# A convolution in the transform domain: two GpSimd sums wait for a later VectorE instruction

## The chip, the cores and the metric

The kernel runs on one core of a Trainium2 chip. A core has five engines, each with its own queue of instructions: TensorE (matmuls and the loads of their stationary operand; PE and PEld in the profile), VectorE (DVE), ScalarE (ACT), GpSimd (POOL) and SyncE (SP, which here only issues DMAs). Engines wait for each other through semaphores: a counter that an instruction raises when it is done, and that another engine's instruction waits for at a given value. The metric is the device time of one execution in microseconds, as the median of several executions.

## The reference

The input x is one image of 224 x 224 pixels with 96 channels, w is a 7 x 7 kernel from 96 to 96 channels, both in bf16. The reference pads w to 224 x 224, transforms both along height and width, multiplies per frequency over the channels, and transforms back:

```python
wp = jnp.pad(w, ((0, H - K), (0, W - K), (0, 0), (0, 0)))
Xf = rfft2(x.astype(float32), axes=(1, 2))
Wf = rfft2(wp.astype(float32), axes=(0, 1))
Yf = jnp.einsum('bhwi,hwio->bhwo', Xf, Wf)
y = irfft2(Yf, s=(H, W), axes=(1, 2)).astype(bfloat16)
```

This is a circular convolution of the image with the 7 x 7 kernel.

## The kernel before

The height is cut into 8 blocks of 28 rows (`NJ`, `B`), the width into 7 tiles of 32 pixels. Along the height a block is taken into a short transform with 17 pairs of components (`NS`), by matmuls with the matrix `Fm`; the result is `xf`. The weights are taken into the same transform by matmuls with `wq`; the result is `WF`, in slots of three parts for each pair: the first two, and their difference, which VectorE makes (`diff` in `prep_jobs`, one bf16 subtraction of 96 x 960 for each pair). Along the width the convolution stays direct, in a form that makes two output columns at a time out of differences and sums of the even and odd columns, the planes `J`. A burst of three VectorE instructions (`jit`) makes the planes of up to three pairs.

A round (t, s) makes the products of tile t for pair s (`b_round`). For an inner pair it is this. Nineteen matmuls into one PSUM bank, b0; ScalarE takes three fifths of it into `tt_`; VectorE takes the rest and makes `u`. Then come jobs of other stages (`mid`: matmuls for the weights or pixels of later rounds, their evictions, and the weight differences). Fourteen matmuls go into a second bank, b1, and VectorE makes `v` from it. Then come the round's plane burst, if it has one (`planes`), and at last the sum of v and u into `yf`, by GpSimd in most rounds:

```python
if not ydve:
    y = ysum(GE)
    if last is not None:
        tc.add_manual_dep(y.ins, last.ins.name, SYNC, reason="sum after planes")
```

The sum of a round with a burst so waits for the burst's last instruction, that of a round without one for its own v. The rounds with pair 0 and the last pair have a single VectorE instruction that writes `yf`, and no sum.

The first two tiles are worked on together: the second follows the first by four rounds (`LAG`). Around the change the order is (0,3), (0,4), (1,0), (0,5), (1,1): first-tile round 3 has a burst (buffer J_66 in the program), round (0,4) has three weight differences in its jobs, round (1,0) has a burst (J_64).

The order on each engine is written out by hand: a wrapper (`_Ordered`) ties each instruction to the one before it on its engine. The tiles u, v and `tt_` have two buffers each, so u of one inner round waits for the sum of the inner round two before it. PSUM has eight banks of 512 floats, handed out in turn as they are emptied; a group of matmuls waits for the eviction of the bank that it takes. `yf` holds three rounds and is stored by one DMA on SP's queue when the third sum is done.

All instructions that go through the wrapper carry its line (L88) in the profile, so that tiles' names and times tell them apart. By the tile of ScalarE's output, the rounds around the change are: (0,3) tt__920, (0,4) tt__1041, (1,0) tt__1107, (0,5) tt__1159, (1,1) tt__1240.

Of the kernel before, what the change touches and what calls it, by code (L numbers as in the profile page):

```python
# [38 lines left out]
JGB = ((0, 3), (3, 6), (6, 9), (9, 12), (12, 15), (15, 17))  # L39
# [5 lines left out]
FI = 6  # L45
LROUND = {8: 16, 11: 15}
WARM0 = 2
BIAS = 2000.0


# [5 lines left out]
def kernel(  # L56
# [18 lines left out]
    SYNC = mybir.DependencyInfo(mybir.DependencyClass.Sync, mybir.DependencyReason.DATA)  # L75
# [19 lines left out]
    VE, SE, GE, TE, DE = (_Ordered(e) for e in (nc.vector, nc.scalar, nc.gpsimd, nc.tensor, nc.sync))  # L95
# [426 lines left out]
        return ops  # L522

    yf_cur = {}

    def pairs(ap):
        return ap.rearrange("p (r g o) -> p g r o", r=2, o=2)
# [4 lines left out]
    def b_round(t, s, mid, end, ydve=False, planes=()):  # L532
        xf = xf_tiles[t][0:C]
        Jb = jbuf[(t, s)]
        xv = xf.rearrange("c p r s w j -> c p r s (w j)")
        st = {
            0: (Jb[:, 4], xv[:, 0, 1, s], xv[:, 0, 0, s]),
            1: (Jb[:, 6], Jb[:, 3], Jb[:, 2]),
            2: (Jb[:, 5], Jb[:, 1], Jb[:, 0]),
        }  # L540
        if t == TL:
            yt, i = (YA, 2 * s) if s < SA else (YB, 2 * (s - SA))
            ym = yt[:, :, i:i + 2, :].rearrange("p g r o -> p g (r o)")
        else:
            for (y0, y1) in YGRP:
                if s == y0:
                    yf_cur[t] = (yf_pool.tile([128, YMAX, 2, 2, C], BF16, name="yf"), y0, y1)
            yf, y0, y1 = yf_cur[t]
            ym = yf[:, s - y0].rearrange("p r m o -> p m r o")

        def conv(bank, col, m, part, add=False, both=False):
            pl = st[m][part] if s not in REAL else (xv[:, 0, :, s], Jb[:, 2:4], Jb[:, 0:2])[m][:, part]
            tp = TAPS[m]
            for k, tp_ in enumerate(tp):
                o, wv = bank[:, col:col + C], WF[0:C, slot(s, part), tp_, :]
                if both:
                    o, wv = bank[:, col:col + 2 * C].rearrange("p (m o) -> p m o", m=2), wv.unsqueeze(1).to_broadcast([C, 2, C])
                TE.matmul(o, lhsT=pl[:, (HALO - k) * NJ:(HALO - k) * NJ + 128], rhs=wv,
                          start=(k == 0 and not add), stop=(k == len(tp) - 1 and not both and m != 2 or not add and not both and k == len(tp) - 1))
        b0, b1 = bank(), bank()  # L560
        merge = t < 2 and s in MERGE
        tt_ = tv_pool.tile([128, 4 * C], F32, name="tt_")
        if s in REAL:
            for part in range(2):
                conv(b0, part * C, 0, part)
            if t == TL:
                SE.copy(out=tt_.rearrange("p (r m o) -> p r m o", r=2, m=2),
                        in_=b0[:, 0:2 * C].rearrange("p (r o) -> p r o", o=C).unsqueeze(2).to_broadcast([128, 2, 2, C]))
            else:
                SE.copy(out=tt_[:, 0:2 * C], in_=b0[:, 0:2 * C])  # L570
            mid()
            for mi, m in enumerate((2, 1)):
                for part in range(2):
                    conv(b1, (part * 2 + mi if t == TL else mi * 2 + part) * C, m, part)
            if t == TL:
                VE.tensor_tensor(out=yp(ym), in0=pairs(tt_[:]), in1=pairs(b1[:, 0:4 * C]), op=ALU.add)
            else:
                VE.tensor_tensor(out=ym,
                                 in0=tt_[:, 0:2 * C].rearrange("p (r o) -> p r o", o=C).unsqueeze(1).to_broadcast([128, 2, 2, C]),
                                 in1=b1[:, 0:4 * C].rearrange("p (m r o) -> p m r o", m=2, r=2), op=ALU.add)  # L580
            load["a"] += 110 + 0.9 * 192
            load["v"] += 540
            for f in planes:
                f()
            end()
        else:
            v = tv_pool.tile([128, 2, 2, C], F32, name="v")
            if merge:
                conv(b0, 2 * C, 0, 0, both=True)
                conv(b0, 2 * C, 2, 0, add=True)  # L590
                conv(b0, 3 * C, 1, 0, add=True)
                conv(b0, 0, 0, 1)
                conv(b0, C, 0, 2)
                SE.mul(out=tt_[:], in_=b0[:, 0:4 * C], mul=-0.5)
                u, pr = tt_[:, 2 * C:4 * C].rearrange("p (m o) -> p m o", m=2), tt_[:, 0:2 * C]
            else:
                for part in range(3):
                    conv(b0, part * C, 0, part)
                conv(b0, 3 * C, 2, 0)
                conv(b0, 4 * C, 1, 0)  # L600
                u = tv_pool.tile([128, 2, C], F32, name="u")
                if t == TL:
                    SE.mul(out=tt_[:, 0:C], in_=b0[:, 0:C], mul=-0.5)
                    SE.copy(out=tt_[:, C:3 * C], in_=b0[:, C:3 * C])
                    load["a"] += 240
                else:
                    SE.mul(out=tt_[:, 0:3 * C], in_=b0[:, 0:3 * C], mul=-0.5)
                pr = tt_[:, C:3 * C]
            if not merge:
                VE.scalar_tensor_tensor(out=u[:], in0=b0[:, 3 * C:5 * C].rearrange("p (m o) -> p m o", m=2), scalar=-0.5,  # L610
                                        in1=tt_[:, 0:C].unsqueeze(1).to_broadcast([128, 2, C]), op0=ALU.mult, op1=ALU.add)
            mid()
            for mi, m in enumerate((2, 1)):
                for pi, part in enumerate((1, 2)):
                    conv(b1, (pi * 2 + mi if t == TL else mi * 2 + pi) * C, m, part)
            if t == TL:
                VE.tensor_tensor(out=v[:], in0=pr.rearrange("p (r o) -> p r o", r=2).unsqueeze(2).to_broadcast([128, 2, 2, C]),
                                 in1=b1[:, 0:4 * C].rearrange("p (r m o) -> p r m o", r=2, m=2), op=ALU.add)
            else:
                VE.scalar_tensor_tensor(out=v.rearrange("p m r o -> p m (r o)"),  # L620
                                        in0=pr.unsqueeze(1).to_broadcast([128, 2, 2 * C]), scalar=-2.0,
                                        in1=b1[:, 0:4 * C].rearrange("p (m q) -> p m q", m=2), op0=ALU.mult, op1=ALU.add)
            def ysum(eng):
                if t == TL:
                    return eng.tensor_tensor(out=yp(ym), in0=pairs(v.rearrange("p r m o -> p (r m o)")),
                                             in1=u.rearrange("p m (g o) -> p (m g) o", o=2).unsqueeze(2).to_broadcast([128, C, 2, 2]), op=ALU.add)
                return eng.tensor_tensor(out=ym, in0=v[:],
                                         in1=u.unsqueeze(2).to_broadcast([128, 2, 2, C]), op=ALU.add)
            if ydve:
                ysum(VE)  # L630
            last = None
            for f in planes:
                last = f()
            if not ydve:
                y = ysum(GE)
                if last is not None:
                    tc.add_manual_dep(y.ins, last.ins.name, SYNC, reason="sum after planes")
            load["a"] += 490 if merge else 410
            load["v"] += (560 if ydve else 250 if t < 2 else 0) + (560 if merge else 900)
            end()  # L640
        if t != TL and s == y1 - 1:
            dma(scr_tiles[t].rearrange("w j s e -> (w j) s e")[:, y0:y1], yf[:, 0:y1 - y0].rearrange("p s r m o -> p s (r m o)"))
# [130 lines left out]
    last = [f() for f in fj[0][1]]  # L773
# [8 lines left out]
    tv_pool = ctx.enter_context(tc.tile_pool(name="tv", bufs=2))  # L782
    load["v"], load["a"] = BIAS, 0.0

# [25 lines left out]
    bursts = {}  # L810
# [7 lines left out]
    nburst = len(bursts)  # L818
    for r in range(NS + LAG):
# [31 lines left out]
        for t in range(2):  # L851
            s = r - LAG * t
# [3 lines left out]
            now = jit(*now) if now else ()  # L856
            both = LAG <= r < NS
            b_round(t, s, fills(qs, 2 * r + (t if both else 0)), fills(qs, 2 * r + (t if both else 1)), False, now)
    assert not bursts and nburst == 2 * len(JGB)
    if NP2:  # L860
        ps0_cm.__exit__(None, None, None)
        ps_cms = [tc.tile_pool(name="ps", bufs=NP2, space=bass.MemoryType.PSUM),
# [42 lines left out]
    turn_b()  # L905
    load["v"] = 2 * BIAS + load["a"]
    for f in cj:
# [20 lines left out]
    order = [(j, h) for j in range(NJ) for h in range(2)]  # L928
    warm(WARM0)
    live = {k: first(*k) for k in order[:FI]}  # L930
    LF = 4
    for i, (j, h) in enumerate(order):
# [3 lines left out]
        k = i + 8 - LF  # L936
# [38 lines left out]
```

## Time and profile before

| | us |
|---|---|
| median of 3 runs (lowest, highest) | 262.58 (261.45, 262.92) |
| the profiled execution, whole | 261.39 |
| its span, first to last instruction | 259.7 |
| TensorE busy in the span | 250.1 |
| VectorE busy | 213.8 |
| ScalarE busy | 197.9 |
| GpSimd busy | 107.8 |
| mean granted TensorE clock | 0.996 |

Times in the views are microseconds from the start of the span. A row of the timeline has the start, the time taken, the engine, the line, the operation, the tiles (out<-in), the shape, and how many instructions of a kind stand in the row; in brackets the engine's idle time before it and what ended that. Consecutive VectorE instructions overlap in the records by 0.08 us. A row of waits has who waited for whom, the total, the number of times and the longest.

### The profile page before, as it was taken

The numbers are of one execution on the slowest core, as the hardware profiler recorded it, in microseconds if no ns is written. First come the engines' busy times: TensorE is split into PE (matmuls) and PEld (weight loads), VectorE is DVE, ScalarE is ACT, GpSimd is POOL, SyncE is SP. The second block draws the span as 40 slices with busy tenths as digits, with TensorE's granted clock in tenths as the row PEclk, the third lists the DMA queues.
The fourth block names the chain that finished last, engine by engine and source line by source line (L and its number), as shares of the span: only waits on it lengthen the run. The fifth ranks groups of instructions, "written<-read, shape, count | busy, mean of one in ns | idle before, by whom it ended". The sixth has DMA issues, their size and how long they took to land.

```text
span 259.7 us, 12201 instructions
## 1 busy us (share of the span) xinstructions
PE 250.1 (96%) x5156; PEld 234.3 (90%) x5156; DVE 213.8 (82%) x455; ACT 197.9 (76%) x499; POOL 107.8 (42%) x172
## 2 busy tenths in 40 slices
PE   8999998999999999999999999999999999999981
PEld 3679998999999999999999998999999999999961
DVE  5649999798978979977988788777978889889982
ACT  5548997668875667998988879989798886666662
POOL 7784123336446543334133322543133332555621
PEclk9999999999999999999999999999999999999998
DMA  6947010731111299888979549697969853595145
GB/s 166 254 126 208 24 49 3 209 113 48 48 48 61 96 254 194 247 237 254 284 213 231 161 122 301 197 264 159 321 232 208 225 172 135 142 172 165 53 117 177
DMA packets 41416, 43.44 MB, mean 167 GB/s; under 512 B 30836, under 2 KB 33104, under 8 KB 41362
## 3 DMA queue, kind: packets, MB, share of 16 engines
q1 hardware_dynamic: 41044, 41.98, 58.7%
q8 instruction: 40, 0.66, 1.1%
q0 software_dynamic: 192, 0.52, 0.7%
q10 hardware_dynamic: 126, 0.17, 0.2%
q14 instruction: 14, 0.11, 0.1%
HBM read 22.09 MB, written 19.66 MB: 161 GB/s over the span
## 4 chain that ended last, share of the span: by engine, by line
PE 82%; DVE 6%; issue 4%; ACT 3%; POOL 3%; DVEq 0%; POOLq 0%; ACTq 0%
PE pb L88 82%; POOL ct L88 2%; DVE J L88 2%; ACT WF L88 1%; DVE xf L88 1%; DVE u L88 1%; POOL yf L88 1%; DVE v L88 1%; DVE WF L88 1%; ACT xf L88 1%; DVE wq L88 1%; DVE yf L88 0%; ACT tt L88 0%; ACT tt__1860 L88 0%; ACT tt__1159 L88 0%
## 5 line engine op out<-in xcount | busy, mean ns | idle before, releaser
L88 PE MATMUL pb<-WF,J 96*128 96x96 bf16 x2782 | 160.4, 206 | 0.1
L88 PEld LDWEIGHTS <-J 96*128 96x128 bf16 x2782 | 136.5, 98 | 7.0 <-issue 0.2
L88 POOL TENSOR_TENSOR yf<-v,u 128x384 bf16<-128x384 f32 x70 | 69.8, 1011 | 124.1 <-issue 67.8
L88 ACT CAST xf<-pb 96x408 bf16<-96x408 f32 (+2 forms) x147 | 68.8, 487 | 8.7 <-PE pb L88 6.9
L88 PE MATMUL pb<-WF,xf 96*128 96x96 bf16 x991 | 61.4, 206 | 0.8 <-ACT xf L88 0.5
L88 DVE TENSOR_TENSOR J<-xf 96x1824 bf16<-96x1824 bf16 (+1 forms) x82 | 56.8, 732 | 0.1
L88 PEld LDWEIGHTS <-xf 96*128 96x128 bf16 x991 | 48.9, 98 | 1.4 <-ACT xf L88 0.6
L88 PE MATMUL pb<-Fm,xn 118*128 118x136 bf16 (+3 forms) x640 | 45.5, 199 | 0.8 <-DVE u L88 0.8
L88 ACT CAST WF<-pb 96x480 bf16<-96x480 f32 (+1 forms) x57 | 28.4, 579 | 4.7 <-PE pb L88 4.6
L88 PE MATMUL pb<-tt,Gm 102*84 102x384 bf16 (+1 forms) x132 | 32.0, 325 | 0.0
L88 PEld LDWEIGHTS <-xn 118*128 118x128 bf16 x640 | 30.5, 97 | 1.1 <-issue 1.0
L88 ACT CAST yo<-pb 84x384 bf16<-84x384 f32 (+1 forms) x65 | 27.8, 484 | 2.8 <-PE pb L88 2.8
L88 ACT CAST J<-pb 84x384 bf16<-84x384 f32 (+1 forms) x65 | 28.0, 484 | 2.5 <-PE pb L88 2.5
L88 DVE TENSOR_TENSOR J<-J 96x912 bf16<-96x912 bf16 (+2 forms) x41 | 22.8, 556 | 0.0
L88 PE MATMUL pb<-wq 98*128 98x120 bf16 (+1 forms) x288 | 21.3, 226 | 0.2 <-DMA wq<-wq 0.2
L88 PEld LDWEIGHTS <-wq 98*128 98x128 bf16 x288 | 19.4, 148 | 0.7 <-issue 0.7
L88 POOL TENSOR_TENSOR xn<-v,u 128x384 bf16<-128x384 f32 x12 | 10.9, 925 | 9.2 <-DVE J L88 6.2
L88 DVE CAST WF<-pb 96x480 bf16<-96x480 f32 (+1 forms) x15 | 8.8, 614 | 4.2 <-PE pb L88 4.0
L88 PE MATMUL pb<-wu 128*128 128x512 bf16 x39 | 10.8, 438 | 1.1 <-DVE ct L88 1.1
L88 DVE TENSOR_TENSOR yf<-v,u 128x384 bf16<-128x384 f32 x20 | 11.2, 558 | 0.7
L88 PEld LDWEIGHTS <-Gm 102*84 102x84 bf16 (+1 forms) x132 | 11.4, 118 | 0.2
L88 ACT COPY xf<-xf 96x816 bf16<-96x816 bf16 (+3 forms) x18 | 10.3, 630 | 0.0
(406 smaller groups left out, 253.5 us busy)
## 6 DMA issues: line engine op xcount, KB each, us to landing
scr<-yf SPq DMA_DIRECT2D x30, 288.0 KB
xn<-in_x_dram SPq DMA_DIRECT2D x12, 672.0 KB
tt<-scr SPq DMA_DIRECT2D x24, 336.0 KB
out_dram<-yo SPq DMA_DIRECT2D x12, 252.0 KB
out_dram<-J SPq DMA_DIRECT2D x12, 252.0 KB
tt<-scr SPq DMA_DIRECT2D x6, 288.0 KB
WF<-in_x_dram SPq DMA_DIRECT2D x2, 672.0 KB
scr<-yf SPq DMA_DIRECT2D x6, 192.0 KB
```

Of the source, the lines that this page charges most:

```text
L88: r = fn(*a, **k)
```

## The change

Two of GpSimd's sums are emitted later in the program, and each waits for the VectorE instruction that was emitted last at that point. The sum of round (0,3) is emitted in round (0,4), behind the three weight differences, and waits for the last of them instead of the burst of its own round. The sum of round (0,4) is emitted in round (1,0), behind the burst, and waits for its last instruction instead of v of its own round. All other sums stay as they were. In the built program each engine has the same instructions in the same order as before; the values that these two sums wait for on VectorE's counter go from 69 to 74 and from 75 to 79, and nothing else differs.

```diff
+YLATE = {(0, 3): 0, (0, 4): 1}
...
+    later = []
+
+    def settle(kind):
+        for k, f in list(later):
+            if k == kind:
+                later.remove((k, f))
+                f(VE._last)
...
             mid()
+            settle(0)
...
             for f in planes:
                 f()
+            settle(1)
             end()
...
             mid()
+            settle(0)
...
             for f in planes:
                 last = f()
-            if not ydve:
+            settle(1)
+
+            def pool_sum(after):
                 y = ysum(GE)
-                if last is not None:
-                    tc.add_manual_dep(y.ins, last.ins.name, SYNC, reason="sum after planes")
+                if after is not None:
+                    tc.add_manual_dep(y.ins, after.ins.name, SYNC, reason="sum after VectorE")
+            if (t, s) in YLATE:
+                later.append((YLATE[(t, s)], pool_sum))
+            elif not ydve:
+                pool_sum(last)
```

More of the change, by code (lines that the diff above doesn't have):

```diff
@@ L858 @@
             b_round(t, s, fills(qs, 2 * r + (t if both else 0)), fills(qs, 2 * r + (t if both else 1)), False, now)
-    assert not bursts and nburst == 2 * len(JGB)
+    assert not bursts and nburst == 2 * len(JGB) and not later
     if NP2:
```

## The prediction

> **What bounds the kernel now.** I read the page first, then the waits of TensorE over the steady part, then the timeline around the two sums. The page, and the stretch of 53 to 247 us with busy time by engine (PE, PEld, DVE, ACT, POOL, each with its instruction count, then the granted clock, the DMA share and GB/s):
>
> ```profile
> span 259.7 us, 12201 instructions
> PE 250.1 (96%) x5156; PEld 234.3 (90%) x5156; DVE 213.8 (82%) x455; ACT 197.9 (76%) x499; POOL 107.8 (42%) x172
> 53.00:247.00 194.00, 193.53 (x4077) 185.54 (x4075) 164.71 (x349) 154.67 (x403) 79.40 (x84) 1.00 0.65 177
> ```
>
> TensorE is busy for 193.53 of the 194.00 us behind the place of the change, at a granted clock of 1.00. So TensorE's stream of matmuls sets the end, and a stall taken out of it earlier should arrive at the end nearly whole. Its waits between 36 and 247 us are one group, and its timeline shows the larger one (an idle time of the engine and what ended it stand in brackets):
>
> ```profile
> PE pb L88 <- DVE u L88: 1.1, 2, 0.8
> ```
>
> ```profile
> 41.83 0.92 PE L88 MATMUL pb<-wq 98*128 98x120 bf16 x12
> 43.51 0.95 PE L88 MATMUL pb<-Fm,xn 118*128 118x32 bf16 x32 [0.76 <-DVE u L88]
> ...
> 45.70 0.92 PE L88 MATMUL pb<-wq 98*128 98x120 bf16 x12
> 46.46 0.56 PE L88 MATMUL pb<-Fm,xn 118*128 118x32 bf16 x16
> ```
>
> Two waits make 1.1 us, and the one at 43.51 is 0.76 of it. The undisturbed pace stands two rows lower: from the twelve weight matmuls to the pixel matmuls behind them it is 46.46 - 45.70 = 0.76 us from start to start. By that pace the matmuls of 43.51 could have started at 41.83 + 0.76 = 42.59, so the stall costs at most 0.92 us. It ended on VectorE's u of first-tile round 5 (tile tt__1159), so VectorE and GpSimd before it are to be read:
>
> ```profile
> 37.42 0.34 DVE L88 SCALAR_TENSOR_TENSOR u<-pb,tt__1041 128x192 f32<-128x192 f32 x1
> 37.69 2.14 DVE L88 TENSOR_TENSOR WF<-WF 96x960 bf16<-96x960 bf16 x3
> 39.75 0.54 DVE L88 SCALAR_TENSOR_TENSOR v<-tt__1041,pb 128x384 f32<-128x384 f32 x1
> 40.22 0.54 DVE L88 TENSOR_TENSOR yf<-tt__1107,pb 128x384 bf16<-128x384 f32 x1
> 40.68 1.96 DVE L88 TENSOR_TENSOR J<-xf 96x1824 bf16<-96x1824 bf16 x2
> 42.56 0.62 DVE L88 TENSOR_TENSOR J<-J 96x912 bf16<-96x912 bf16 x1
> 43.11 0.34 DVE L88 SCALAR_TENSOR_TENSOR u<-pb,tt__1159 128x192 f32<-128x192 f32 x1
> 43.38 0.54 DVE L88 SCALAR_TENSOR_TENSOR v<-tt__1159,pb 128x384 f32<-128x384 f32 x1
> 43.84 0.34 DVE L88 SCALAR_TENSOR_TENSOR u<-pb,tt__1240 128x192 f32<-128x192 f32 x1
> 44.10 0.64 DVE L88 CAST WF<-pb 96x480 bf16<-96x480 f32 x1
> ```
>
> ```profile
> 37.18 1.00 POOL L88 TENSOR_TENSOR yf<-v,u 128x384 bf16<-128x384 f32 x1 [3.82 <-DVE J L88]
> 40.37 1.00 POOL L88 TENSOR_TENSOR yf<-v,u 128x384 bf16<-128x384 f32 x1 [2.19 <-DVE v L88]
> 43.99 1.00 POOL L88 TENSOR_TENSOR yf<-v,u 128x384 bf16<-128x384 f32 x1 [2.63 <-DVE v L88]
> ```
>
> VectorE has no idle time in these rows: it is behind, and every tenth it saves before 43.11 moves u forward. The first two GpSimd rows are the sums of first-tile rounds 3 and 4, the third is that of round 5. The sum of round 3 (37.18 to 38.18) lies over the weight differences that start at 37.69; that of round 4 (40.37 to 41.37) over the plane burst that starts at 40.68. What this does, taken apart in narrow windows:
>
> ```profile
> 37.69 1.01 DVE L88 TENSOR_TENSOR WF<-WF 96x960 bf16<-96x960 bf16 x1
> 38.62 0.64 DVE L88 TENSOR_TENSOR WF<-WF 96x960 bf16<-96x960 bf16 x1
> ...
> 28.96 1.10 DVE L88 TENSOR_TENSOR J<-xf 96x1824 bf16<-96x1824 bf16 x1
> ...
> 40.68 1.65 DVE L88 TENSOR_TENSOR J<-xf 96x1824 bf16<-96x1824 bf16 x1
> ...
> 51.86 1.02 DVE L88 TENSOR_TENSOR WF<-WF 96x960 bf16<-96x960 bf16 x1
> ...
> 235.86 1.22 DVE L88 TENSOR_TENSOR J<-xf 96x1824 bf16<-96x1824 bf16 x1
> ```
>
> ```profile
> 50.41 1.96 POOL L88 TENSOR_TENSOR yf<-v,u 128x384 bf16<-128x384 f32 x2 [3.65 <-DVE J L88]
> ...
> 235.20 0.92 POOL L88 TENSOR_TENSOR xn<-v,u 128x384 bf16<-128x384 f32 x1 [0.43 <-DVE xf L88]
> ```
>
> A difference takes 0.64 without a sum beside it and 1.01 at 37.69; the first burst instruction takes 1.10 alone (28.96) and 1.65 at 40.68. Overlap against excess in the four places: 38.18 - 37.69 = 0.49 against 0.37; 41.37 - 40.68 = 0.69 against 0.55; 52.37 - 51.86 = 0.51 against 0.38; 236.12 - 235.86 = 0.26 against 0.12. The excess is each time the overlap less 0.12 to 0.14: the VectorE instruction is held almost until the running sum ends. I use "overlap less 0.13".
>
> **The change part by part.** All engines keep their instructions and their order; two GpSimd sums wait for a later VectorE instruction. Nothing is added or removed, and no DMA moves in its queue.
>
> 1. The sum of round 3 leaves the weight differences: the first falls from 1.01 to 0.64 or 0.65, and VectorE gains 0.36 (the overlap of 0.49 less 0.13). The differences end at 37.69 + 2.14 - 0.36 = 39.47 instead of 39.83. A sum starts 0.08 after its release (v ends at 40.29, sum at 40.37), so it runs from 39.55 to 40.55.
>
> 2. What it now lies beside: v of round 4 (from 39.39) and the second tile's first yf (from 39.86), each with one operand in PSUM. The yf row of 40.22 lay beside a sum from 40.37 on and took 0.54, the same as v at 39.75, which ended before that sum began; so I price these two at nothing. If v were held to the moved sum's end, less the 0.13, it would end at 40.42 instead of 39.93 and the gain would fall by 0.49 to 0.32; no row has such an instruction held.
>
> 3. The burst starts at 40.68 - 0.36 = 40.32, with 40.55 - 40.32 = 0.23 of the moved sum still to run. By overlap less 0.13 that costs 0.10, near the 0.12 of the row at 235.86 with almost the same overlap. The ends are 0 and the whole 0.23. The sum of round 4 is gone from it (0.55). Net 0.45 in the burst, with ends of 0.32 and 0.55.
>
> 4. Together u of round 5 starts 0.36 + 0.45 = 0.81 sooner, at 42.30, and ends at 42.64 instead of 43.45. TensorE started 0.06 behind that end (43.51), so its pixel matmuls start at 42.70, 0.81 sooner and 0.11 above the 42.59 that its own pace allows. With the ends of step 3 the gain is 0.68 to 0.91, and the pace caps it at 0.92.
>
> 5. What waits for the moved sums. u of round 5 writes the buffer that the sum of round 3 reads: that sum ends at 40.55, u starts at 42.30, so 1.75 is to spare. u of second-tile round 1 (tt__1240) writes the buffer that the sum of round 4 reads. That sum is released by the burst's end, 43.18 - 0.81 = 42.37, and runs 42.45 to 43.45. VectorE is at this u at 43.84 - 0.81 = 43.03 and now stands idle to about 43.48, taking the 0.03 after a sum's end from this pair:
>
> ```profile
> 57.51 1.03 POOL L88 TENSOR_TENSOR yf<-v,u 128x384 bf16<-128x384 f32 x1 [1.95 <-issue]
> 58.57 0.36 DVE L88 SCALAR_TENSOR_TENSOR u<-pb,tt__1653 128x192 f32<-128x192 f32 x1 [0.47 <-POOL yf L88]
> ```
>
> That is a new wait of 0.45, yet u starts 0.36 sooner than before (43.48 against 43.84). Its PSUM bank is taken next by the weight matmuls of 45.70, which move to 44.89; u ends at 43.82, 1.07 earlier. Queued behind it is the weight eviction of 44.10, now 43.74 to 44.38, whose bank is wanted at 45.65 (46.46 less 0.81). So it costs nothing.
>
> 6. GpSimd's queue: behind the sum of round 4 stands that of round 5, at 43.45 instead of 43.99; the store of rounds 3 to 5 on SP's queue waits for this one and can go 0.54 sooner. ScalarE works from the same banks:
>
> ```profile
> 40.41 0.41 ACT L88 ACTIVATE tt__1159<-pb 128x288 f32<-128x288 f32 x1 [1.23 <-PE pb L88]
> 42.07 0.77 ACT L88 CAST xf<-pb 96x320 bf16<-96x320 f32 x2
> ```
>
> The activation of 40.41 follows v of round 4 (end 40.29) and moves forward 0.36 with it; the evictions of 42.07 end at 42.48, and TensorE wants their banks from 43.10 (half of the pixel matmuls behind 42.70). Nothing is late there.
>
> The sum: -0.81 us. The profiled execution took 261.39 us (1.69 outside its span) and would take 260.58. It lies 1.19 under the median of 262.58; set against the median the prediction is 261.8. That is 0.3%, and a measurement of this kernel can tell about 0.5% from no change.
>
> The Trainium skill's page "SBUF — State Buffer", section "Who interferes with whom", has a rule that speaks partly against the change: a VectorE instruction with two SBUF inputs and a GpSimd instruction that reads SBUF exclude each other, and whichever issues first keeps the port for its whole length. The trace agrees but for the 0.13. By the rule taken whole, the burst of step 3 loses 0.23 and the gain is 0.68; by the rows it is 0.81.
>
> **The rivals.** (a) The moved sum holds the burst for the whole 0.23: step 4 gives 0.68, 261.9 us. Against it stand the four rows that are 0.12 to 0.14 short. (b) No gain: VectorE's lead is used up elsewhere, for instance because the sum of round 3 starts late and lies wholly over the burst. At a start of 40.3 it would hold the burst for 0.87, u of round 5 would gain 0.36 + 0.55 - 0.87 = 0.04, and the time would be 262.5. For it speaks that the sum's end and the burst's start are only 0.23 apart; against it that the lag from release to start would have to be 0.8 where the rows show 0.08. (c) Slower: the sum of round 4, now last before u of tt__1240, becomes TensorE's wait. This decides once the sum ends past 43.45 + 1.07 = 44.52, and it is slower than before past 45.33. The longest of the 70 sums took 1670 ns:
>
> ```profile
> L88 POOL TENSOR_TENSOR yf<-v,u x70: 992/1000/1670, 31.1 to 220.3; 128x384 bf16<-128x384 f32 x70
> ```
>
> With that length it ends at 44.12, still in time. It needs a second such delay and 1.3 us more to be past the band; at an end of 46.0 the time would be 262.58 + 0.67 = 263.3.
>
> **How the numbers follow.** Forecast (gain 0.7 to 0.9) 0.66; (a) 0.12; (b) 0.14; (c) 0.08. The likeliest is 261.8; its own range is 261.6 to 262.1. The range reaches up to (b) and the highest run of before (262.9), and down to the profiled run less the cap, 261.39 - 0.92 = 260.5, since the runs of before spread from 261.45 to 262.92 and three new ones may gather at the fast end. Beyond 0.5% (1.31 us) no step leads; the scatter of two medians gives 0.16 of faster. Slower is (c), 0.08. Within the band is left 0.76.
>
> **What would show it.** Right: in the profile after, the first difference behind u of tt__1041 takes 0.64, the burst's first instruction 1.1 to 1.25, u of tt__1159 starts 0.7 to 0.9 sooner, TensorE's idle time of 0.76 is gone or under 0.15, and u of tt__1240 has a new wait of some 0.4 on GpSimd. Wrong: the burst still takes 1.6 (b), TensorE waits for u of tt__1240 (c), or the stall is gone and the span is not shorter, which would mean that a later stall takes it back.

## The result and the profile after

The changed kernel takes 260.68 us (median of 22 runs, 260.36 to 263.80) where the kernel before, run beside it, takes 261.75 us (22 runs, 260.98 to 263.33). The ratio is 0.9964, with a 95% interval of 0.9949 to 0.9978: 0.94 us less, between 0.58 and 1.33 (the plain difference of the two medians is 1.07). The whole interval lies below 1, so the change is faster; its size lies within the 0.5% band that the prediction spoke of.

The profiled execution of the changed kernel is no shorter than that of before (261.59 against 261.39 us whole, span 259.8 against 259.7), and it has to be seen why before the spans are compared. The rows are TensorE's first matmuls on the transposed weights, before and after:

```profile
15.68 0.49 PE L88 MATMUL pb<-wq 98*128 98x128 bf16 x5 [0.21 <-DMA wq<-wq]
```

```profile
16.49 0.50 PE L89 MATMUL pb<-wq 98*128 98x128 bf16 x5 [0.88 <-DMA wq<-wq]
```

In this execution the weights landed later and TensorE began this work 0.81 us later. Over the profiles of this study that start lies anywhere from 15.36 to 16.55, so a single span says nothing about a gain of 0.8. The landing is not the only thing that moves it: in the second profile of the changed kernel this work begins at 15.41, and the place of the change is reached no sooner (42.63 against 42.64). What follows compares stretches inside the profiles. VectorE and GpSimd of the changed kernel around the two sums (tt__1040 is here the tile that was tt__1041):

```profile
38.22 0.34 DVE L89 SCALAR_TENSOR_TENSOR u<-pb,tt__1040 128x192 f32<-128x192 f32 x1
38.48 1.77 DVE L89 TENSOR_TENSOR WF<-WF 96x960 bf16<-96x960 bf16 x3
40.19 0.54 DVE L89 SCALAR_TENSOR_TENSOR v<-tt__1040,pb 128x384 f32<-128x384 f32 x1
40.65 0.54 DVE L89 TENSOR_TENSOR yf<-tt__1106,pb 128x384 bf16<-128x384 f32 x1
41.12 1.51 DVE L89 TENSOR_TENSOR J<-xf 96x1824 bf16<-96x1824 bf16 x2
42.55 0.62 DVE L89 TENSOR_TENSOR J<-J 96x912 bf16<-96x912 bf16 x1
43.10 0.34 DVE L89 SCALAR_TENSOR_TENSOR u<-pb,tt__1159 128x192 f32<-128x192 f32 x1
43.36 0.53 DVE L89 SCALAR_TENSOR_TENSOR v<-tt__1159,pb 128x384 f32<-128x384 f32 x1
44.29 0.36 DVE L89 SCALAR_TENSOR_TENSOR u<-pb,tt__1240 128x192 f32<-128x192 f32 x1 [0.39 <-POOL yf L89]
```

```profile
40.34 1.02 POOL L89 TENSOR_TENSOR yf<-v,u 128x384 bf16<-128x384 f32 x1 [6.17 <-DVE WF L89]
43.25 1.97 POOL L89 TENSOR_TENSOR yf<-v,u 128x384 bf16<-128x384 f32 x2 [1.90 <-DVE J L89]
```

The three differences take 1.77 instead of 2.14, the first two instructions of the burst 1.51 instead of 1.96. The first of each, in narrow windows (before they took 1.01 and 1.65):

```profile
38.48 0.64 DVE L89 TENSOR_TENSOR WF<-WF 96x960 bf16<-96x960 bf16 x1
...
41.12 1.21 DVE L89 TENSOR_TENSOR J<-xf 96x1824 bf16<-96x1824 bf16 x1
```

From the start of the differences to u of round 5 VectorE now needs 43.10 - 38.48 = 4.62 us, where it needed 43.11 - 37.69 = 5.42. The sums stand where the change puts them: the first behind the last difference, the second behind the burst, that of round 5 right behind it. TensorE, the same two rows as before:

```profile
42.64 0.91 PE L89 MATMUL pb<-wq 98*128 98x120 bf16 x12
43.49 0.95 PE L89 MATMUL pb<-Fm,xn 118*128 118x32 bf16 x32
```

From start to start these are 0.85 us apart, 0.09 more than the undisturbed 0.76; before it was 1.68, or 0.92 more. So 0.83 of the stall is gone, and the idle time of 0.76 with it. Behind it the shape of the work is unchanged: from the pixel matmuls to the end the two profiles have 216.19 and 216.31 us, and between 53 and 247 us

```profile
53.00:247.00 194.00, 193.56 (x4085) 185.79 (x4083) 164.44 (x349) 154.50 (x402) 78.36 (x84) 1.00 0.64 178
```

TensorE is busy for 193.56 of 194.00, as it was for 193.53. The gain is not taken back later. The one new thing is a gap of TensorE at 52.71 us:

```profile
52.71 0.88 PE L89 MATMUL pb<-WF,J 96*128 96x96 bf16 x17 [0.25 <-issue]
```

No wait of the profile ends it; the second profile of the same kernel, below, does not have it, nor does any other.

### The profile page after: what moved, and what is told of

The parts are those of the page before. It is cut to its first block, busy times and chain, and to the rows that moved or that the text cites. A ratio compares the mean times of both kernels' runs of the same rounds, so it can differ in the third digit from the quotient of the medians.

```text
span 259.8 us, 12201 instructions
## 1 busy us (share of the span) xinstructions
PE 250.4 (96%) x5156; PEld 234.3 (90%) x5156; DVE 213.0 (82%) x455; ACT 197.9 (76%) x499; POOL 107.1 (41%) x172
## 4 chain that ended last, share of the span: by engine, by line
PE 81%; DVE 6%; DMA 4%; issue 3%; ACT 2%; SPq 2%; POOL 0%; DVEq 0%; ACTq 0%
PE pb L89 81%; DMA wq<-in_w_dram 2%; DVE J L89 2%; DMA wq<-wq 2%; SPq L89 2%; ACT WF L89 1%; DVE v L89 1%; DVE xf L89 1%; DVE WF L89 1%; DVE u L89 1%; ACT xf L89 1%; POOL yf L89 0%; DVE yf L89 0%; ACT tt L89 0%; ACT tt__1860 L89 0%
## 5 line engine op out<-in xcount | busy, mean ns | idle before, releaser
L89 PE MATMUL pb<-wu 128*128 128x512 bf16 x39 | 11.4, 456 | 1.1 <-DVE ct L89 1.1
L89 PEld LDWEIGHTS <-wu 128*128 128x128 bf16 x39 | 4.3, 114 | 7.0 <-issue 3.3
```

The costliest lines, as they stand in the source:

```text
L89: r = fn(*a, **k)
```

## The experiments

All variants keep every engine's order of instructions, except where it is said. They were timed in two groups, each beside its own runs of the kernel before, so that ratios are compared and not times. In the table, "stall" is the start-to-start time from the twelve weight matmuls to the pixel matmuls behind them, less 0.76. It is read in one profile each and does not depend on when the weights land.

| kernel | first difference | burst's first | stall | ratio to before, 95% interval |
|---|---|---|---|---|
| before | 1.01 | 1.65 | 0.92 | |
| changed | 0.64 | 1.21 | 0.09 | 0.9964 (0.9949 to 0.9978) |
| changed, again | 0.64 | 1.22 | 0.02 | 0.9964 (0.9940 to 0.9987) |
| first sum only | 0.65 | 1.22, then 1.21 | 0.94 | 0.9994 (0.9969 to 1.0019) |
| second sum only | 1.01 | 1.09 | 0.35 | 0.9977 (0.9951 to 1.0004) |
| first sum behind v | 0.65 | 1.66 | 0.56 | 0.9977 (0.9954 to 1.0001) |
| memsets for the sums | 0.65 | 1.10 | under 0.02 | 0.9971 (0.9958 to 0.9984) |
| second sum later still | 0.65 | 1.22 | 0.11 | 0.9970 (0.9954 to 0.9986) |
| both sums behind the burst | 0.65 | 1.10 | 0.41, 0.8 us later | 0.9988 (0.9971 to 1.0004) |
| first sum at the second difference | 0.65 | 1.10 | under 0.02 | 0.9983 (0.9968 to 0.9997) |

The intervals do not tell most neighbours apart; the order of the variants rests on the rows. The ratios do not follow that order everywhere: the last version has one of the smallest stalls, yet its time is 0.44 us (0.08 to 0.84) below before, less than the 0.9 of stall that is gone from its profile. No run here says why.

**The changed kernel again.** No edit.

> The changed kernel once more, for its time beside the variants and for a second profile. Hold theory (a VectorE instruction with two bf16 operands in SBUF is held until a running GpSimd sum ends, less some 0.13 us): first difference 0.64, first burst instruction 1.1 to 1.25, pixel matmuls behind the twelve weight matmuls after at most 0.15 us of stall, 0.7 to 0.9 us faster than before. The stall of 0.41 at 52.71 us in the first profile after: if the change makes it, it stands here again; if it is chance, it does not.

The rows came out so, and the gap at 52.71 does not come with the change: in this profile the 25 matmuls across that place run through.

```profile
42.63 0.92 PE L89 MATMUL pb<-wq 98*128 98x120 bf16 x12
43.41 0.95 PE L89 MATMUL pb<-Fm,xn 118*128 118x32 bf16 x32
...
51.84 1.23 PE L89 MATMUL pb<-WF,J 96*128 96x96 bf16 x25
```

**The parts alone.** The first sum only, then the second only:

```diff
-YLATE = {(0, 3): 0, (0, 4): 1}
+YLATE = {(0, 3): 0}
```

```diff
-YLATE = {(0, 3): 0, (0, 4): 1}
+YLATE = {(0, 4): 1}
```

> Only the sum of round 3 is moved behind the weight differences; the sum of round 4 waits for its own v as before. Hold theory: the differences gain 0.36, but the two sums now run one after the other, the second from about 0.2 behind the burst's start to 1.2 behind it, so the burst's first instruction is held for 1.0 to 1.1 instead of 0.55 and takes 2.1 to 2.2. u of round 5 comes 0.1 to 0.2 later than before, TensorE's idle time is 0.85 to 0.95 instead of 0.76, and the time is 0.1 to 0.2 us above before. Rival (the differences alone carry the gain): 0.36 us faster.

> Only the sum of round 4 is moved behind the burst; the sum of round 3 lies over the differences as before. Hold theory: first difference 1.01, first burst instruction 1.10, u of round 5 0.55 sooner, TensorE's idle time about 0.2 instead of 0.76, 0.5 to 0.6 us faster than before. Rival (the two parts only work together): no change.

VectorE, GpSimd and TensorE with the first sum alone:

```profile
37.98 1.78 DVE L89 TENSOR_TENSOR WF<-WF 96x960 bf16<-96x960 bf16 x3
...
40.61 1.22 DVE L89 TENSOR_TENSOR J<-xf 96x1824 bf16<-96x1824 bf16 x1
...
41.75 1.21 DVE L89 TENSOR_TENSOR J<-xf 96x456 bf16<-96x456 bf16 x1
```

```profile
39.84 1.02 POOL L89 TENSOR_TENSOR yf<-v,u 128x384 bf16<-128x384 f32 x1 [6.19 <-DVE WF L89]
...
40.82 1.88 POOL L89 TENSOR_TENSOR yf<-v,u 128x384 bf16<-128x384 f32 x1
```

```profile
42.12 0.91 PE L89 MATMUL pb<-wq 98*128 98x120 bf16 x12
43.82 0.93 PE L89 MATMUL pb<-Fm,xn 118*128 118x32 bf16 x31 [0.79 <-DVE u L89]
```

The differences gain their 0.37, and all of it is lost again in the burst: the stall is 0.94 against 0.92. That nothing would be gained was expected, though not the size (0.85 to 0.95 of idle time, where it is 0.79), and the way was another: the burst's first instruction was to take 2.1 to 2.2 and took 1.22. The second sum did not hold the burst's first instruction, which was running when it came. It was itself held and took 1.88 instead of 1.00; when the first instruction ended the sum had its turn, and the burst's second instruction, 0.38 otherwise, took 1.21. So the hold goes both ways, and changes hands between two VectorE instructions.

The second sum alone behaves as expected, with 0.20 of idle time and 0.35 of stall against 0.92 before:

```profile
38.03 1.01 DVE L89 TENSOR_TENSOR WF<-WF 96x960 bf16<-96x960 bf16 x1
...
41.03 1.09 DVE L89 TENSOR_TENSOR J<-xf 96x1824 bf16<-96x1824 bf16 x1
```

The first sum's move is worth nothing alone, but 0.26 to 0.33 on top of the second (0.35 less 0.09 or 0.02): the parts don't add.

**The first sum a little later.**

```diff
-YLATE = {(0, 3): 0, (0, 4): 1}
+YLATE = {(0, 3): 1, (0, 4): 1}
```

> The sum of round 3 is released by v of round 4 instead of by the last difference, some 0.46 us later; the sum of round 4 is behind the burst as in the changed kernel. Hold theory: the sum of round 3 lies 0.69 over the burst, whose first instruction takes 1.65 again; only the 0.36 of the differences is gained, TensorE's idle time is 0.4, and the time is 0.3 to 0.4 us below before and 0.45 above the changed kernel. Rival (it matters only that the sums are out of the differences and that the sum of round 4 is out of the burst): as the changed kernel.

```profile
40.99 1.66 DVE L89 TENSOR_TENSOR J<-xf 96x1824 bf16<-96x1824 bf16 x1
```

```profile
40.68 1.00 POOL L89 TENSOR_TENSOR yf<-v,u 128x384 bf16<-128x384 f32 x1 [6.66 <-DVE v L89]
```

```profile
42.50 0.91 PE L89 MATMUL pb<-wq 98*128 98x120 bf16 x12
43.82 0.95 PE L89 MATMUL pb<-Fm,xn 118*128 118x32 bf16 x32 [0.40 <-DVE u L89]
```

The sum ends at 41.68, so it lies 0.69 over the burst's first instruction, which takes 0.56 more than 1.10; TensorE's idle time is the expected 0.40. Sizes follow "overlap less 0.13" here too.

**Is it the reading?** The kernel before, with the two sums left out and three memsets of the same part of `yf` in place of each:

```diff
-                y = ysum(GE)
+                if (t, s) in ((0, 3), (0, 4)):
+                    for _ in range(3):
+                        y = GE.memset(ym, 0.0)
+                        tc.add_manual_dep(y.ins, VE._last.ins.name, SYNC, reason="sum after planes")
...
```

> The kernel before, in which the two GpSimd sums are left out: each is replaced by three memsets of the same part of yf (0.4 us each, some 1.2 together, so that they lie over the differences and over the burst as the sums did), released as the sums were before. The output lacks these two rounds. If the hold comes from GpSimd reading SBUF: no hold, first difference 0.64, first burst instruction 1.10, u of round 5 is 0.9 sooner, TensorE's stall behind the twelve weight matmuls is gone, 0.8 to 1.0 us faster than before, at or just under the changed kernel. If any GpSimd instruction holds: first difference 0.9 to 1.4, first burst instruction 1.5 to 2.0, and the stall stays at 0.5 or more.

```profile
37.38 0.65 DVE L88 TENSOR_TENSOR WF<-WF 96x960 bf16<-96x960 bf16 x1
...
40.01 1.10 DVE L88 TENSOR_TENSOR J<-xf 96x1824 bf16<-96x1824 bf16 x1
```

```profile
36.85 1.37 POOL L88 MEMSET yf<- 128x384 bf16 x3 [3.66 <-DVE J L88]
39.69 1.37 POOL L88 MEMSET yf<- 128x384 bf16 x3 [1.46 <-DVE v L88]
```

The memsets lie over the first difference until 38.22 and over the burst until 41.06, longer than the sums did, and neither is held. The memsets are not stretched either: all six take 0.42. A GpSimd instruction that only writes does no harm here. A sum differs from a memset in more than its reading, but the profile of before has a GpSimd copy, which reads a single operand and adds nothing, over a VectorE instruction with two operands in SBUF:

```profile
22.19 0.77 DVE L88 TENSOR_TENSOR J<-J 96x608 bf16<-96x608 bf16 x1
```

```profile
22.04 0.59 POOL L88 COPY xf<-xf 96x384 bf16<-96x384 bf16 x1
```

The same form takes 0.46 at 36.63, with no GpSimd instruction beside it; here it takes 0.30 more for an overlap of 0.44 with the copy. So what holds VectorE is the reading. The Trainium skill's page "SBUF — State Buffer", section "Who interferes with whom", says the same: two SBUF inputs on VectorE contend with a GpSimd instruction that reads SBUF, "not with one that only writes it"; the trace agrees, 0.65 and 1.10. This variant also gives the ceiling, a stall under 0.02; the changed kernel leaves 0.02 to 0.09 of it, and their ratios are not told apart.

**How late may the second sum be?** It waits for v of round 5 (`settle(2)` stands behind v):

```diff
-YLATE = {(0, 3): 0, (0, 4): 1}
+YLATE = {(0, 3): 0, (0, 4): 2}
...
+            settle(2)
             def ysum(eng):
```

> The changed kernel, but the sum of round 4 waits for v of round 5 instead of for the burst, some 0.7 us later. Slack theory (the delayed sum has about 1.07 us to spare before TensorE wants the bank that u of second-tile round 1 empties): u of tt__1240 waits about 1.1 instead of 0.4 on GpSimd, TensorE has no new wait, and the time is that of the changed kernel, 0.7 to 0.9 us below before. Rival (the wait of u is already on the path): 0.5 to 0.7 us slower than the changed kernel, with a TensorE wait on this u.

```profile
44.62 0.36 DVE L89 SCALAR_TENSOR_TENSOR u<-pb,tt__1240 128x192 f32<-128x192 f32 x1 [1.11 <-POOL yf L89]
```

VectorE's wait grows from 0.39 to 1.11, and the profile lists no wait of TensorE between 40 and 53 us; the stall is 0.11, near the 0.09 of the changed kernel, and the ratios are not told apart. The slack that the prediction worked out is real: in the changed kernel this u ends at 44.65, 1.04 before the weight matmuls that take its bank (45.69), and here at 44.98, still 0.32 before them (45.30).

**Both sums behind the burst**, the first one too:

```diff
-YLATE = {(0, 3): 0, (0, 4): 1}
+YLATE = {(0, 3): 2, (0, 4): 1}
...
             for f in planes:
                 f()
+            settle(2)
             settle(1)
```

> Both sums are moved behind the burst: no hold at all, but u of round 5 has to wait for the sum of round 3, which now ends about 1.0 behind the burst. Hold theory: differences 0.64, burst 1.10, then VectorE idles some 0.7 to 1.0 before u of round 5, which ends about 0.3 later than before. In this program the bank that u empties is taken by matmuls 0.8 later in TensorE's order than in before, so TensorE waits about 0.4 there instead of 0.92: 0.4 to 0.6 us faster than before, 0.3 to 0.4 slower than the changed kernel. Rival (free VectorE work is all that counts): as the changed kernel or better.

```profile
43.32 0.36 DVE L89 SCALAR_TENSOR_TENSOR u<-pb,tt__1159 128x192 f32<-128x192 f32 x1 [1.12 <-POOL yf L89]
```

```profile
42.53 0.96 PE L89 MATMUL pb<-Fm,xn 118*128 118x32 bf16 x32
43.74 0.93 PE L89 MATMUL pb<-WF,J 96*128 96x96 bf16 x18 [0.25 <-DVE u L89]
```

No hold is left, but u of round 5 waits 1.12 for the sum, a little more than the 0.7 to 1.0 expected, and TensorE for u. The pixel matmuls take 0.80 from start to start (43.51 to 44.30 in before), so 43.74 is 0.41 late. This is not a clean comparison with before: as the expectation says, the bank that this u empties goes here to the next group of matmuls, and not to the pixel matmuls. Had these still needed it, they could not have started before 43.74 either, 1.21 behind their 42.53 (an estimate from these rows), which is more than the 0.92 of before. VectorE's free time is not all that counts; the buffer's next writer has to get its sum in time.

**The first sum while the differences still run.** It waits for the second difference (the differences are kept in a list, `made`):

```diff
-                f(VE._last)
+                f(VE._last if kind else made[-2])
```

> The changed kernel, but the sum of round 3 waits for the second of the three differences, so that it is released while the third runs. If the instruction that runs first keeps the other out, whichever engine it is on: the sum is recorded 0.5 sooner and lasts 1.4 to 1.6, the third difference takes 0.64, the burst's first instruction 1.10 to 1.15, and the time is that of the changed kernel or 0.1 below. If a sum always holds VectorE: the third difference takes 1.0 to 1.5, u of round 5 comes some 0.4 later than in the changed kernel, TensorE's stall is 0.4 to 0.6.

```profile
39.68 0.65 DVE L89 TENSOR_TENSOR WF<-WF 96x960 bf16<-96x960 bf16 x1
...
41.18 1.10 DVE L89 TENSOR_TENSOR J<-xf 96x1824 bf16<-96x1824 bf16 x1
```

```profile
39.84 1.39 POOL L89 TENSOR_TENSOR yf<-v,u 128x384 bf16<-128x384 f32 x1 [5.61 <-DVE WF L89]
```

Here the third difference runs first: it takes its 0.65, and the sum, recorded from 39.84, is stretched to 1.39. It ends at 41.23, only 0.05 into the burst, and the stall is gone. By its rows this version is at the ceiling and ahead of the changed kernel by under 0.1 us. Its measured ratio (0.9983, 0.9968 to 0.9997) does not bear that out; the interval overlaps that of the changed kernel.

## Why the prediction was right

The predicted 261.8 us lay on a median of 262.58 from three runs. Over 22 runs before is at 261.75; the 0.81 of the forecast taken from that is 260.94, against 260.68 measured. So the base was 0.83 high, and the change itself measured 0.94 (0.58 to 1.33) where 0.81 was forecast.

The mechanism and the size of the change were right; that the time itself was hit has a share of luck. The measured 260.68 lies below the forecast's own 261.6 to 262.1, and 0.18 inside the low end of the wide range (260.5), which the prediction had stretched downwards because the three runs of before spread so far. The measurement also told 0.36% from no change, where the prediction had counted on about 0.5%.

One of the prediction's signs of being wrong came by its letter: the stall is gone and the span of the first profile is not shorter (259.8 against 259.7). It does not mean what the prediction says: no later stall takes the gain back, as the stretch behind the change shows. A span also holds the start of the program, and so was the wrong thing to watch.

Step 1, the differences: 0.64 for the first as forecast, 0.37 gained (2.14 to 1.77).

Step 2, the work the moved sum now lies beside: v and yf take 0.54 each beside the sum of 40.34 to 41.36. Priced at nothing, cost nothing. The row that the prediction leaned on could not show it, since that yf (40.22) had started before its sum (40.37). Here yf starts at 40.65, 0.31 behind the sum's start, and is not held.

Step 3, the burst: the moved sum overlaps it by 41.36 - 41.12 = 0.24 and its first instruction takes 1.21, 0.11 more than alone; 0.10 was forecast. This decides against rival (a), which has the whole overlap as the loss, by 0.13 us in the row. In the variant with the sum behind v, an overlap of 0.69 gives 0.56; in before it gave 0.55.

Step 4, the stall: 0.09 left in the first profile and 0.02 in the second, where 0.11 was forecast.

Step 5, the new wait: 0.39 where 0.45 was forecast, and it costs TensorE nothing. The slack of 1.07 held when a further 0.72 of it was used up (1.11 - 0.39), which rules out rival (c) at this size. Whether the last 0.3 of it holds too was not tried.

Step 6, the queues: with the profile's shift of 0.79 (38.48 - 37.69) taken off, the second sum starts at 42.46 where 42.45 was forecast.

Rival (b), no gain through a sum that lies over the burst, fails by the same rows: the release took 0.08 (the last difference ends at 40.26, the sum starts at 40.34). Where the sum was made to start 0.47 later on purpose, so that 0.69 of it lay over the burst, 0.47 of the gain of 0.83 was lost (a stall of 0.56 against 0.09). In the rival's own sum the hold should be 0.85 and not 0.87 (a sum of 40.3 to 41.30 over a burst from 40.32, less 0.13); its 262.5 stays.

That TensorE's stream would carry the gain to the end is shown by the times of the changed kernel; by the profiles alone it is not, since the start of the program moves their spans by more than the gain.

Two things the prediction did not use: that a sum can be the one that is held, and that the hold changes hands inside a burst. Both bear on variants, and on one row that it quotes. The sum of 1670 ns, which rival (c) takes as a delay that could hit any sum, lay beside a burst in the profile of before:

```profile
87.34 0.78 DVE L88 TENSOR_TENSOR J<-xf 96x1216 bf16<-96x1216 bf16 x1
88.04 1.04 DVE L88 TENSOR_TENSOR J<-xf 96x152 bf16<-96x152 bf16 x1
```

```profile
87.32 1.67 POOL L88 TENSOR_TENSOR yf<-v,u 128x384 bf16<-128x384 f32 x1
```

The burst's first instruction takes the 0.78 that it takes alone, the sum 0.67 more than its 1.00, and the second instruction 1.04, where this form takes 0.23 alone. That is the pattern of the variant with the first sum alone, and it was there to be read before the change. The moved sum of round 4 has no instruction with two operands in SBUF beside it and takes 1.00.

Why the excess falls 0.11 to 0.14 short of the overlap is open; the records give starts and ends of whole instructions, and no run here takes the reading apart from them.

## What to carry to other kernels

Two engines that look independent in the program can hold each other, here a VectorE instruction with two operands in SBUF and a GpSimd instruction that reads SBUF: compare the duration of one instruction with and without the other engine beside it, and take the overlap of their rows against the excess. Where the holding instruction has slack, a later wait on it can give the other engine its time back at no cost, but only if the place that it moves to is free of the same conflict and the buffer's next writer still gets it in time. Moved by half, it takes the loss along. A gain of a few tenths of a per cent is read in the start-to-start times around the stall, not in the span of one profile.

## What the runs showed of the hardware

A VectorE instruction with two bf16 operands in SBUF was held by a running GpSimd sum until nearly its end (0.36 for an overlap of 0.49, 0.11 for 0.24). The reverse held too: a GpSimd sum that came while such an instruction ran was stretched from 1.00 to 1.39 in one variant and to 1.88 in another, and in the second it went ahead of the VectorE instruction next in line, which then took 1.21 instead of 0.38. A GpSimd copy held VectorE as a sum did (0.30 for 0.44 at 22.19 in before). "Overlap less 0.13" is not a rule for every pair: beside another copy in before, at 165.87, a burst instruction lost 0.08 for an overlap of 0.37. GpSimd memsets held nothing (0.65 and 1.10 beside them), and a VectorE instruction with one operand in PSUM was not held (0.54 beside a sum and without).

The Trainium skill's page "SBUF — State Buffer", section "Who interferes with whom", gives the rule that whichever issues first keeps the port for its whole instruction. In these variants the instruction that started second is the one that lost time, which agrees with it; where the two records start only 0.02 apart, at 87.32 in before, they do not settle the order. The size of the loss does not quite agree, on either side. The VectorE instructions beside sums lose 0.11 to 0.14 less than the full overlap, and the stretched sums of 1.39 and 1.88 lose 0.10 and 0.12 less (0.39 for an overlap of 0.49, 0.88 for 1.00).
